# A decode kernel (GQA attention and MLP): the second piece of wo goes through ScalarE's DMA queue

## The chip, the core and the metric

The kernel runs on one core of one Trainium2 chip. The metric is the device time of one execution in microseconds (us). The engines are named as in the profile: PE is TensorE's matmuls and PEld its weight loads, DVE is VectorE, ACT is ScalarE, POOL is GpSimd and SP is SyncE. SPq and ACTq are those engines' sequencers, which also issue DMAs. All times in the text are counted from the start of the profiled span.

## The reference: what is computed

One token x of 512 values passes a layer norm. The result goes two ways, and both are added to x.

```python
xn = _layernorm(x, axis=-1)
return x + _A_ref(xn, A_k_cache, A_v_cache, A_wq, A_wo) + _B_ref(xn, B_w1, B_w2)
```

`_A_ref` is attention of one query position over a cache of 65536 positions: 32 query heads and 8 key/value heads of 128 values (four query heads share a key/value head), softmax, and the product with `wo`, a matrix of 4096 x 512. `_B_ref` is `relu(xn @ w1) @ w2` with 1792 hidden values. Everything is float32. The two caches hold 537 MB, the weights 24 MB.

## The kernel before

The whole kernel is written by hand: every engine has its own program, with semaphore waits where it needs another's result. Two large buffers in SBUF take all loads, `ks` and `vs`, each 128 partitions x 64 KB.

**Start.** SP loads wq into `vs` in two pieces and the first part of K into `ks`; ScalarE loads x twice, 2 KB each. The layer norm and the product with wq give the queries.

**The loop of 32 steps** (8 heads x 4 parts). SP loads a part of K (8 MB) into `ks`, and a part of V (8 MB) into `vs`, as soon as the buffer is free: lines 294 to 299, with the semaphores `k_free` and `v_free`. TensorE multiplies K by the queries (L329), VectorE transposes the scores out of PSUM and takes maxima (L361 to L378), ScalarE makes the exponentials (L407), TensorE multiplies them with V (L345), and VectorE takes the result out of PSUM (L383 to L390). L383 raises `v_free` when the step's last matmul with V is done.

**The end of SP's program** sets the order of the last loads. After the last part of V stand w1 and w2 (3.5 MB each, into `ks`), then a wait for `v_free` to reach 32, and then wo into `vs`. wo is cut into 32 slices of 512 columns, each 2 KB a row, and loaded in six pieces of 16, 8, 4, 2, 1 and 1 slices (`WO`). All this is in one queue. `load_slices` (L158) issues the pieces with `load` (L150), each with a semaphore of its own, and returns for every slice the semaphore of its piece.

**The tail of TensorE.** After the loop it multiplies by w1 (L428), transposes the hidden values (L269), sums the softmax's denominators (L439), scales the attention's output and puts it in order (L453, L461). VectorE makes `sw`, the 32 columns of attention output (L465, L472). Then one chain of products is gathered in PSUM, `gather` at L480 to L487: 14 slices of w2, then the slices 0 to 23 of wo, each waiting for its own piece. L498 copies this sum to SBUF, L501 folds it into `acc_y`, and L510 adds slices 24 to 31 there. L516 adds x, and SP writes y.

```python
for j in range(SLICES):
    row = vs[:, j * D : (j + 1) * D]
    lhsT = sw[:, j : j + 1]
    if j < DIRECT:
        gather(j % CT, lhsT, row, [sw_in, wo_in[j]], last=(j >= DIRECT - CT))
```

TensorE runs its instructions in the order in which they are written, so slice j is multiplied before slice j + 1, whichever piece landed first. ScalarE has nothing to do after its loop (L403 to L420).

Of the kernel before, what the change touches and what calls it, by code (L numbers as in the profile page):

```python
# [30 lines left out]
STEPS = HKV * NP  # L31
# [3 lines left out]
R = HKV  # L35
SLICES = R * G
WQ = [4, 28]
WO = [16, 8, 4, 2, 1, 1]
# [30 lines left out]
def attention_and_mlp_kernel(  # L69
# [29 lines left out]
    te, ve, se, ge, sy = nc.tensor, nc.vector, nc.scalar, nc.gpsimd, nc.sync  # L99
# [4 lines left out]
    def place(name, *shape):  # L104
        return sb.tile([P, *shape], F32, name=name)

    ks = place("ks", NT * KEYS)
    vs = place("vs", NT * KEYS)
# [34 lines left out]
    with tc.tile_critical():  # L143
# [6 lines left out]
        def load(engine, name, dst, src, n=16):  # L150
            sem = nc.alloc_semaphore(name)
            engine.dma_start(dst, src).then_inc(sem, n)
            return sem, n
# [1 line left out]

        x_in = load(se, "x_in", xT, x.rearrange("(p a) -> p a", p=P))

        def load_slices(name, src, counts):  # L158
            marks = []
            for n in counts:  # L160
                cut = slice(len(marks) * D, (len(marks) + n) * D)
                marks += [load(sy, f"{name}{len(marks)}", vs[:, cut], src[:, cut])] * n
            return marks

        def k_part(i):
# [3 lines left out]
        def v_part(i):  # L169
            h, n = divmod(i, NP)  # L170
            src = v[h].rearrange("(p t b) d -> p t (b d)", p=P, b=SUB)
            return src[:, n * NT : (n + 1) * NT, :].rearrange("p t f -> p (t f)")

        wq_in = load_slices("wq", wq.rearrange("h (i r) a f -> (h i) (r a f)", r=R), WQ)
        sy.dma_start(ks, k_part(0)).then_inc(k_in, 16)

# [125 lines left out]
        w1_in = load(sy, "w1_in", t1, w1.rearrange("p a f -> p (a f)"))  # L302
        w2_in = load(sy, "w2_in", t2, w2.rearrange("p j n -> p (j n)"))
        sy.wait_ge(v_free, STEPS)
        wo_in = load_slices("wo", wo.rearrange("h (i r) g f -> (h i) (r g f)", r=R), WO)


        ge.wait_ge(*q_made)
# [13 lines left out]
        with nc.Fori(0, STEPS, engines=[ENG.PE]):  # L322
            te.wait_ge(k_in, 16).then_inc(k_in, -16)
            te.wait_ge(q_in, 1).then_inc(q_in, -1)  # L324
            for s in range(NT):
                pt = (pa, pb)[s // 2 % 2][:, s % 2, :]
                for c in range(CT):
                    at = (s * CT + c) * TW
                    i = te.matmul(pt[32 * c : 32 * c + 32, :], qcur, ks[:, at : at + TW], start=True, stop=True)  # L329
# [12 lines left out]
            n = NT * SUB // WIDE  # L342
# [12 lines left out]
        with nc.Fori(0, HKV, engines=[ENG.DVE]):  # L355
            for n in range(NP):
                for s in range(0, NT, 2):
                    if s == NT - 2:

                        ve.wait_ge(s_tiles, NT // 2).then_inc(k_free, 1)  # L360
                    i = ve.transpose(  # L361
                        tr[:, s * SUB : (s + 2) * SUB, :].rearrange("p b i -> p (b i)"),
                        (pa, pb)[s // 2 % 2].rearrange("p i k -> p (i k)"),
                    )._wait_ge(s_tiles, s // 2 + 1)
# [5 lines left out]
                i = ve.reduce_max(top, tr[:, :, :G].rearrange("p b g -> p g b"), axis=AX.X)  # L370
                if n:
                    ve.drain()
                    i = ve.tensor_max(m, m, mc)  # L373
# [29 lines left out]
        with nc.Fori(0, HKV, engines=[ENG.Activation]):  # L403
            for n in range(NP):
                se.wait_ge(s_bias, 1).then_inc(s_bias, -1)  # L405
                for g in range(G):
                    i = se.activation(  # L407
                        wt[:, :, g], tr[:, :, g], AF.Exp, bias=bias[:, n, g : g + 1],
                        scale=scale, accum_out=part[:, n, g : g + 1],
                    )  # L410
                i.then_inc(s_w, 1)
                if n:
                    se.activation(
                        alpha[:, n : n + 1], bias[:, n - 1, G : G + 1], AF.Exp,
                        bias=bias[:, n, G : G + 1], scale=-1.0,
                    ).then_inc(s_alpha, 1)
            se.wait_ge(s_diff, 1).then_inc(s_diff, -1)
            se.activation(
                fac.rearrange("p n g -> p (n g)"), diff.rearrange("p n g -> p (n g)"), AF.Exp
            ).then_inc(s_alpha, 1)  # L420


        w = t1.rearrange("p (a f) -> p a f", a=A)
# [127 lines left out]
```

## Time and profile before

| | |
|---|---|
| time, median of 3 runs | 1305.26 us (1304.88 to 1305.73) |
| the profiled execution | 1305.38 us |
| its span, first to last instruction | 1303.3 us |
| bytes read from memory | 560.99 MB, 430 GB/s over the span |
| PE busy | 662.4 us (51%) |
| DVE busy | 268.9 us (21%) |
| ACT busy | 75.9 us (6%) |
| granted TensorE clock, mean | 0.734 |

The page gives busy shares of each engine and, in 40 slices of the span, the share of the DMA engines. The DMA lines give for each load its size and the time from its issue to its landing. The timeline lists instructions in order of time: start, duration, engine, line, operation, what it writes and reads, and in brackets how long the engine sat idle before it and what ended that. A granted clock of 0.5 means that TensorE runs at half speed.

### The profile page before, as it was taken

What the parts mean: (1) busy time and instruction counts of PE and PEld (TensorE: products, weight loads), DVE (VectorE), ACT (ScalarE), POOL (GpSimd) and SP (SyncE); (2) the same over time, 40 slices, a digit from 0 to 9 for tenths busy, and PEclk for the clock granted to TensorE, in tenths of its full rate; (3) what the DMA queues carried; (4) which work ended last, traced back from release to release, by engine and by line L of the source; (5) the groups of instructions that cost most, each with busy time, mean ns of one, the idle gap of its engine ahead of it and who ended that gap; (6) DMA issues with size and microseconds to landing.
All of it is one profiled execution on the core that took longest, in us unless ns stands there. A gap on an engine that the chain in (4) does not pass through costs nothing. (4 is left out here: it accounts for less than half of the span.)

```text
span 1303.3 us, 10616 instructions
## 1 busy us (share of the span) xinstructions
PE 662.4 (51%) x4562; PEld 243.2 (19%) x4562; DVE 268.9 (21%) x395; ACT 75.9 (6%) x292; POOL 5.4 (0%) x22
## 2 busy tenths in 40 slices
PE   4355446445445535445545535544544644553657
PEld 2121112112112112111211111221111212111123
DVE  2221122221122222012222112222112222211222
ACT  0000000000000000000000000000000000000000
POOL 0000000000000000000000000000000000000000
PEclk9677687777677677677778677767767666767768
DMA  9999999999999999999999999999999999999998
GB/s 418 419 445 422 447 422 447 420 447 422 440 428 430 438 422 445 424 445 424 445 422 447 422 447 420 443 426 436 432 426 443 424 443 424 445 424 445 422 429 346
DMA packets 10821, 561.06 MB, mean 430 GB/s; under 512 B 1336, under 2 KB 1344, under 8 KB 1728
## 3 DMA queue, kind: packets, MB, share of 16 engines
q1 hardware_dynamic: 10664, 560.99, 99.5%
q8 instruction: 3, 0.05, 0.0%
q10 hardware_dynamic: 152, 0.00, 0.0%
q14 instruction: 2, 0.02, 0.0%
HBM read 560.99 MB, written 0.00 MB: 430 GB/s over the span
## 5 line engine op out<-in xcount | busy, mean ns | idle before, releaser
L345 PE MATMUL acc_o<-vs,wt 128*16 128x512 f32 x2048 | 292.0, 734 | 180.1 <-PEq L341 180.1
L329 PE MATMUL pa<-ks,qcur 128*32 128x512 f32 x1024 | 183.6, 814 | 328.9 <-PEq L324 328.9
L361 DVE STREAM_TRANSPOSE tr<-pa 128x1024 f32<-128x1024 f32 x64 | 80.0, 1250 | 421.4 <-PE pa L329 421.4
L329 PE MATMUL pb<-ks,qcur 128*32 128x512 f32 x1024 | 144.0, 653 | 0.0
L329 PEld LDWEIGHTS pa<-ks,qcur 128*32 128x32 f32 x1024 | 64.3, 133 | 416.2 <-issue 403.7
L345 PEld LDWEIGHTS acc_o<-vs,wt 128*16 128x16 f32 x2048 | 68.9, 113 | 376.4 <-issue 376.4
L407 ACT ACTIVATE wt<-tr,bias 128x128 f32<-128x128 f32 x128 | 64.3, 511 | 1085.3 <-ACTq L405 1085.3
L387 DVE SCALAR_TENSOR_TENSOR acc<-acc,alpha,acc_o 128x512 f32<-128x512 f32 x24 | 17.9, 747 | 352.5 <-PE acc_o L345 352.5
L361 DVE STREAM_TRANSPOSE tr<-pb 128x1024 f32<-128x1024 f32 x64 | 80.0, 1250 | 45.5 <-PE pb L329 45.5
L329 PEld LDWEIGHTS pb<-ks,qcur 128*32 128x32 f32 x1024 | 66.2, 129 | 78.3 <-issue 58.4
L334 PE MATMUL pm<-ident,m 128*4 128x128 f32 x32 | 10.0, 313 | 87.0 <-DVE m L373 66.6
L385 DVE COPY acc<-acc_o 128x512 f32<-128x512 f32 x8 | 5.5, 692 | 118.9 <-PE acc_o L345 118.9
L335 PE MATMUL pm<-dg,ones 4*128 4x4 f32 x64 | 15.0, 302 | 21.4 <-DVE dg L377 21.4
L370 DVE TENSOR_REDUCE mc<-tr 128x4 f32<-128x512 f32 x24 | 24.1, 1006 | 1.8
L334 PEld LDWEIGHTS pm<-ident,m 128*4 128x4 f32 x32 | 2.6, 81 | 116.0 <-DVE m L373 88.4
L407 ACT ACTIVATION_READ_ACCUMULATOR wt<-tr,bias 128x1 f32 x128 | 23.9, 187 | 0.0
L335 PEld LDWEIGHTS pm<-dg,ones 4*128 4x128 f32 x64 | 12.2, 236 | 28.8 <-DVE dg L377 28.8
L336 PE MATMUL pm<-dg,rowg 4*128 4x1 f32 x64 | 14.3, 290 | 0.0
L336 PEld LDWEIGHTS pm<-dg,rowg 4*128 4x128 f32 x64 | 13.0, 249 | 0.0
L278 PE MATMUL pa<-vs,tr 128*8 128x512 f32 x64 | 9.9, 769 | 6.1 <-DMA vs<-wq 4.8
L375 DVE TENSOR_REDUCE mg<-pm 4x1 f32<-4x128 f32 x32 | 8.9, 279 | 13.0 <-PE pm L334 13.0
L378 DVE COPY bias<-pm 128x5 f32<-128x5 f32 x32 | 5.2, 163 | 27.8 <-PE pm L336 27.8
(90 smaller groups left out, 116.6 us busy)
## 6 DMA issues: line engine op xcount, KB each, us to landing
vs<-wq SPq DMA_DIRECT2D x1, 7168.0 KB, 21.4
ks<-w SPq DMA_DIRECT2D x2, 3584.0 KB, 22.1
vs<-wo SPq DMA_DIRECT2D x1, 4096.0 KB, 16.4
vs<-wo SPq DMA_DIRECT2D x1, 2048.0 KB, 20.9
vs<-wq SPq DMA_DIRECT2D x1, 1024.0 KB, 4.9
vs<-wo SPq DMA_DIRECT2D x1, 1024.0 KB, 22.9
ks<-k SPq DMA_DIRECT2D x32, 29.2
vs<-v SPq DMA_DIRECT2D x32, 29.3
```

The lines of the kernel that those rows point to most:

```text
L278: lambda e: e.matmul(pr[32 * c : 32 * c + HKV, :], xs[:, i, :], vs[:, i * 512 : (i + 1) * 512], start=(i < CT), stop=(i >= SLICES - CT),),
L329: i = te.matmul(pt[32 * c : 32 * c + 32, :], qcur, ks[:, at : at + TW], start=True, stop=True)
L334: te.transpose(pm[:G, :P], m, ident)._wait_ge(s_dve, 3).then_inc(s_max, 1)
L335: te.matmul(pm[:, P : P + G], ones[:G, :], dg[:, :G], start=True, stop=True)._wait_ge(s_dve, 4)
L336: te.matmul(pm[:, P + G : P + G + 1], rowg, dg[:, G : G + 1], start=True, stop=True).then_inc(s_max, 1)
L345: mm = te.matmul(acc_o[32 * c : 32 * c + WIDE * G, :], wt[:, i * WIDE : (i + 1) * WIDE, :].rearrange("p b g -> p (b g)"), vs[:, i * 512 : ...
L361: i = ve.transpose(tr[:, s * SUB : (s + 2) * SUB, :].rearrange("p b i -> p (b i)"), (pa, pb)[s // 2 % 2].rearrange("p i k -> p (i k)"),)._ ...
L370: i = ve.reduce_max(top, tr[:, :, :G].rearrange("p b g -> p g b"), axis=AX.X)
L375: ve.reduce_max(mg, pm[:G, :P], axis=AX.X)._wait_ge(s_max, 1)
L385: ve.tensor_copy(flat, acc_o)
L387: ve.scalar_tensor_tensor(flat, flat, alpha[:, n : n + 1], acc_o, op0=ALU.mult, op1=ALU.add)
L407: i = se.activation(wt[:, :, g], tr[:, :, g], AF.Exp, bias=bias[:, n, g : g + 1], scale=scale, accum_out=part[:, n, g : g + 1],)
```

## The change

`load_slices` takes a further argument, the number of a piece that is issued by ScalarE instead of SP. wo is loaded with `other=1`: the second piece, the eight slices from slice 16 on (2 MB, 16 KB a row), is issued by ScalarE, after its loop and after a wait for `v_free`. The other five pieces stay on SP in their order. The call moves behind ScalarE's loop in the text, so that ScalarE's issue comes after its loop; SP's own program keeps its order and its wait. The order of TensorE's work is the same.

```diff
-        def load_slices(name, src, counts):
+        def load_slices(name, src, counts, other=None):
+
             marks = []
-            for n in counts:
+            for i, n in enumerate(counts):
                 cut = slice(len(marks) * D, (len(marks) + n) * D)
-                marks += [load(sy, f"{name}{len(marks)}", vs[:, cut], src[:, cut])] * n
+                engine = se if i == other else sy
+                marks += [load(engine, f"{name}{len(marks)}", vs[:, cut], src[:, cut])] * n
             return marks
...
         sy.wait_ge(v_free, STEPS)
-        wo_in = load_slices("wo", wo.rearrange("h (i r) g f -> (h i) (r g f)", r=R), WO)
...
+        se.wait_ge(v_free, STEPS)
+        wo_in = load_slices("wo", wo.rearrange("h (i r) g f -> (h i) (r g f)", r=R), WO, other=1)
```

## The prediction

> **What bounds the kernel now.** I read the page's slices and queues first, then the DMA issues, then the timeline of the last 30 us with the chain of waits.
>
> ```profile
> DMA  9999999999999999999999999999999999999998
> q1 hardware_dynamic: 10664, 560.99, 99.5%
> ```
>
> The 16 DMA engines are busy to the end, and practically all of it is SP's queue (q1). The packet records say the same more sharply: from 1262 to 1292 us 16.0 transfers are under way in every 2 us. So the last byte can land earlier only if the engines move bytes faster. Loads of one queue land in the order of issue:
>
> ```profile
> vs<-wo SPq DMA_DIRECT2D x1, 4096.0 KB, 16.4
> vs<-wo SPq DMA_DIRECT2D x1, 2048.0 KB, 20.9
> vs<-wo SPq DMA_DIRECT2D x1, 1024.0 KB, 22.9
> vs<-wo SPq DMA_DIRECT2D x1, 512.0 KB, 23.8
> vs<-wo SPq DMA_DIRECT2D x2, 256.0 KB, 24.0
> ```
>
> The six issues begin at 1273.19 and then every 0.37 to 0.49 us. The two weights ahead of them were issued at 1253.40 and 1253.77, and landed 18.0 and 26.1 us later. With the last column this gives the landings: w1 1271.4, w2 1279.9, piece 0 (slices 0 to 15) 1289.6, piece 1 (slices 16 to 23, the one that moves) 1294.5, piece 2 at 1297.0, and the last at 1299.5. Each piece takes a time in proportion to its bytes (9.7, 4.9, 2.5 us): no gap anywhere. TensorE meets them like this:
>
> ```profile
> 1286.69 4.52 PE L483 MATMUL acc_z<-ks,hT 128*1 128x512 f32 x26
> ...
> 1291.05 5.73 PE L483 MATMUL acc_z<-vs,sw 128*1 128x512 f32 x46
> ...
> 1294.54 0.10 PEld L483 LDWEIGHTS acc_z<-vs,sw 128*1 128x1 f32 x6 [0.41 <-DMA vs<-wo]
> ...
> 1296.95 0.69 DVE L498 COPY rows<-acc_z 128x512 f32<-128x512 f32 x1 [9.08 <-PE acc_z L483]
> 1297.69 0.40 PE L501 MATMUL acc_y<-rows,ones 128*1 128x128 f32 x8 [0.91 <-DVE rows L498]
> ...
> 1299.56 0.10 PEld L510 LDWEIGHTS acc_y<-vs,sw 128*1 128x1 f32 x8 [0.23 <-DMA vs<-wo]
> 1300.10 0.29 DVE L516 TENSOR_TENSOR x<-acc_y,x 128x128 f32<-128x128 f32 x1 [2.46 <-PE acc_y L510]
> ```
>
> Columns are start, duration, engine, line. TensorE works through w2's 14 slices, then piece 0, then piece 1, almost without a pause until 1296.78 (1291.05 + 5.73). It waits for piece 1 by less than 0.1 us of lost pace at 1294.54, and for the last piece by 0.12 us at 1299.56 (a group of four that otherwise starts 0.09 us after the one before starts 0.21 after it). So two limits meet here: landings and TensorE's order of slices. TensorE is in order: slice 16 can't run before slice 15. That is what the change disturbs.
>
> **The change part by part.**
>
> *SP loses one issue.* Its four later pieces are issued some 0.45 us earlier. They stand behind 16 us of queued bytes, so this is worth 0. If that cover were gone it would be worth at most the 0.45 us.
>
> *ScalarE gains a wait and one DMA.* Its last activation (L418) ends at 1274.58 and the condition (v_free at 32) was met at 1273.2, so the wait costs nothing; behind it on ScalarE stand only this DMA and the end of the program. An issue lasts 0.33 to 0.44 us in the rows. The load of x at the kernel's start shows the lag: issued by ScalarE at 0.92, its first packets at 1.97, that is 1.05 us. I estimate that piece 1's first rows move at about 1276 (bounds: 1275.6 at once, and 1280 if it takes the 4.7 us that the second load of x took from the end of its issue at 2.46 to its packets at 7.14; that one stood behind the first load's rows in ScalarE's own queue and behind one 56 KB row, and nothing stands ahead here).
>
> *How two queues share an engine.* Before, this happens only in the first 10 us. An engine's eight 16-byte rows of x lie about 0.31 us apart there, each between two 8 KB rows of wq that take 309 ns: the engine alternates row by row. The page's own figure agrees: 2 KB of x took 4.3 us to land beside the first 1024 KB of wq, 4.9 us. Each DMA has 8 rows per engine. Rows take 1.06 us (w2, 28 KB), 1.21 us (piece 0, 32 KB), 0.61 us (piece 1, 16 KB). So from 1276 each row of piece 1 goes between two of SP's. The fast engines have about two rows of w2 left, the slowest about four. Piece 1's eight rows are through after at most eight more rows of SP, which is before the end of piece 0. Piece 1 lands near 1291.5. w2 lands at 1279.9 + 4 x 0.61 = 1282.3 at the latest; its matmuls begin at 1286.69, so those 2.4 us are hidden (cover 4.4 us).
>
> *Piece 0 is the one that pays.* It lands when w2, piece 0 and piece 1 are all through: the sum of bytes that in the run before ended at **1294.5**, instead of 1289.6. Does sharing change the rate? 8 KB rows took 309 ns between the rows of x and 309 to 315 alone at the end, so at most 2% either way; over the 18 us of sharing that bounds it by 0.35 us up or down, and I take 0.
>
> *TensorE.* w2's slices run as before, 1286.69 to about 1291.6. Then TensorE waits some 2.9 us for piece 0 while piece 1 lies ready or nearly so. From 1294.55 it has 24 slices to do instead of 8. The pace at full clock: four instructions, two slices, each 0.43 us (weight loads at 1292.33, 1292.76, 1293.19). 24 slices are 12 such steps; the last starts at 1294.55 + 11 x 0.43 = 1299.28 and lasts 0.59: 1299.87. Before it was 1296.78: **+3.09**. The copy L498, L501 and L510 follow unchanged, only the 0.12 us wait for the last piece goes (it landed at 1299.5, L510 now ends near 1303): **-0.12**. Sum +2.97 us.
>
> *The sum.* The profiled execution took 1305.38 us, its span 1303.3 (2.1 us lie around it); it is 0.12 above the median, 1305.26. 1305.38 + 2.97 = 1308.35, which I give as **1308.3**, against the median +0.23%.
>
> **The TensorE clock in the gap.** In rows: it fell to half at 1279.2 after the window 1275.8 to 1279.2 with TensorE busy 1.50 of 3.40 us, stayed full after 70.9 to 74.3 with 1.43 busy, all matmuls of 512 columns, and fell at 94.8 after 1.13 us.
>
> ```profile
> 1275.80:1279.20 3.40, 1.50 (x12) 0.69 (x6) 2.62 (x6) 0.00 (x0) 1.09 (x1) 1.00 1.02 437
> 1279.20:1282.60 3.40, 3.32 (x16) 3.32 (x16) 0.02 (x1) 0.00 (x0) 0.00 (x0) 0.50 0.98 424
> ...
> 1286.00:1289.40 3.40, 3.40 (x20) 1.17 (x23) 1.04 (x2) 0.00 (x0) 0.00 (x0) 0.50 0.97 414
> 1289.40:1292.80 3.40, 3.40 (x40) 0.70 (x30) 0.00 (x0) 0.00 (x0) 0.00 (x0) 0.99 0.97 410
> ```
>
> (The third number from the end is the granted clock.) The clock moves on a 3.41 us grid. After the change the window 1289.4 to 1292.8 would be busy about 2.2 us and the next, to 1296.2, about 1.7, both above the 1.43 that kept it. So I leave it at full. The Trainium skill ("TensorE: Matmul & The Clock Gate", Part 1) has the clock fall only after a wholly idle window of about 3.4 us; by that the 2.9 us gap is safe and the sum is the same, but the drop at 1279.2 after a window 44% busy speaks against so mild a rule, and it is why the next rival keeps a chance.
>
> **The rivals.**
>
> 1. *The clock falls in the gap.* For: the drops above, and that another execution may have its grid elsewhere. Against: the two windows. From 1294.55 the steps take 0.85 us instead of 0.43 (as at 1287.50 and 1288.35). One cold window of 3.41 us costs half of it, 1.7; a cold stretch to 1299.7 costs 2.6. Time 1310.0 to 1310.9. Chance 0.14.
>
> 2. *Piece 1 is served last*, SP's queue first. Piece 0 lands at 1289.6 as before, the small pieces by 1294.6, piece 1 at 1299.5. Then 8 slices, 4 steps: 1299.55 + 3 x 0.43 + 0.59 = 1301.43 instead of 1296.78, less 0.12: +4.5, 1309.9. Against: the alternating rows of x. Chance 0.04.
>
> 3. *The order in the engines hardly changes: no difference.* Piece 1's rows start late, behind much of piece 0. From a start at about 1280 on (the slowest engine's end of w2), every SP row of 1.21 us that passes first brings piece 0 0.61 us nearer to its old 1289.6. At a start of 1284 piece 0 lands near 1292.5 and piece 1 near 1294 to 1296; the end is then 1305.3 to 1307. For: the second load of x needed 7 us to land. Against: ScalarE is free at 1274.6, and its rows should move four us before the point that decides. If the slowest engines catch up in other executions, piece 0 lands at 1293, TensorE is the limit of the run before too, and the loss shrinks to about 2.2 us, 1307.5: the same side of the bound. The Trainium skill ("DMA: Bandwidth & Descriptors", Queues, rings and completion order) lets an engine take a whole packet of some 9 to 17 descriptors from one queue before it turns to the other. By that piece 1 goes in one turn after w2, and piece 0 still lands at 1294.5; only with a start after 1280 would it come wholly behind piece 0, and the time be 1305.3. The alternating rows above are against it. Chance together 0.17.
>
> 4. *Two queues move bytes faster.* To gain, piece 0 would have to land by 1291.2 and the last by 1297: over 10% more rate in 26 us. Against: engines 99.5% taken, equal 309 ns rows. 1302.5 or less. Chance 0.03.
>
> **How the numbers follow.** Forecast 0.62, rivals 0.14, 0.04, 0.17, 0.03. The forecast's own range is 1307.4 to 1309.2 (0.35 from the rate, the rest from the landing of the slowest engine and from run to run, 1304.88 to 1305.73). A measurement here tells about 0.2%, 2.6 us, from no change, so the bound lies at 1307.87, inside the forecast's lower part: 0.52 of its 0.62 are slower, 0.10 same. Slower 0.52 + 0.14 + 0.04 = 0.70, same 0.27, faster 0.03. The range reaches into rivals 1 and 3: 1306.3 to 1310.3.
>
> **What would show it.** Profile after: the piece of 2048 KB stands at ACTq, with 15 to 18 us to landing; the 4096 KB piece at 21.3 instead of 16.4; a wait of 2.5 to 3 us before slice 0, released by the DMA of wo; L498 starts at 1300.0 relative to the same start; no DMA wait before L510; the last landing unchanged at 1299.5 and the clock at full from 1294.5. Wrong if the 4096 KB piece lands under 19 us (rival 3), if the clock after the gap is 0.5 (rival 1), or if the last landing moves by over 1 us (rival 4).

## The result and the profile after

The changed kernel takes **1310.45 us** in the median of 6 runs (1309.35 to 1311.54), against 1305.30 us before (1304.88 to 1305.73): a ratio of 1.0039, 95% interval 1.0029 to 1.0049. It is slower by 5.2 us, where 3.0 had been forecast and the range ended at 1310.3. The profiled execution took 1310.78 us, its span is 1308.7.

The transfers went as forecast. These are the DMA issues after: size, and time from issue to landing.

```profile
vs<-wo SPq DMA_DIRECT2D x1, 4096.0 KB, 22.7
...
vs<-wo ACTq DMA_DIRECT2D x1, 2048.0 KB, 18.0
...
vs<-wo SPq DMA_DIRECT2D x2, 256.0 KB, 25.9
```

SP's issues begin at 1271.55 here (1273.19 before), so the columns are not compared line by line; added to the issue they are. Piece 0 landed at 1294.24 (before 1289.60), piece 1 at 1290.69 (before 1294.50), the last piece at 1299.28 (before 1299.52). Piece 0 and piece 1 have changed places, and no time was lost or won in the transfers as a whole.

The timeline from the products with the normalised output on:

```profile
1277.48 2.01 PE L458 MATMUL pm<-norm,fins 128*128 128x4 f32 x16 [0.68 <-DVE norm L451]
...
1283.34 4.93 PE L488 MATMUL acc_z<-ks,hT 128*1 128x512 f32 x28
...
1294.38 7.95 PE L488 MATMUL acc_z<-vs,sw 128*1 128x512 f32 x48 [6.11 <-DMA vs<-wo]
...
1302.49 0.69 DVE L503 COPY rows<-acc_z 128x512 f32<-128x512 f32 x1 [17.98 <-PE acc_z L488]
```

(L458 is L453 of before, L488 is L483, L503 is L498.) The wait for piece 0 is there, but it is 6.11 us and not 2.9, and the 48 instructions of the 24 slices last 7.95 us. The chain of waits after says the same in two lines: 22.70 us for the landing, then TensorE.

```profile
1271.55 22.70 DMA vs<-wo
1294.24 0.14 issue
1294.38 8.08 PE acc_z L488 x48
```

The stretches of the clock's grid, the windows of 3.41 us at whose ends the clock changes (TensorE busy is the second number, the granted clock the third from the end):

```profile
1286.10:1289.50 3.40, 2.17 (x16) 0.27 (x8) 0.00 (x0) 0.00 (x0) 0.00 (x0) 1.00 1.06 453
1289.50:1292.90 3.40, 0.00 (x0) 0.00 (x0) 0.00 (x0) 0.00 (x0) 0.00 (x0) 1.00 0.93 398
1292.90:1296.30 3.40, 1.92 (x12) 0.43 (x16) 0.00 (x0) 0.00 (x0) 0.00 (x0) 0.50 0.97 394
1296.30:1299.70 3.40, 3.40 (x20) 0.58 (x16) 0.00 (x0) 0.00 (x0) 0.00 (x0) 0.50 0.38 139
1299.70:1303.10 3.40, 2.63 (x24) 0.38 (x16) 0.61 (x1) 0.00 (x0) 0.00 (x0) 1.00 0.00 0
```

One window passes with TensorE wholly idle, and the clock is at half for the two windows that follow, 1292.9 to 1299.7. From piece 0's landing on, the first 5.3 us of work run at half speed.

The two executions against each other: the gather ended at 1302.33 (1294.38 + 7.95) instead of 1296.78, 5.55 us later, and the profiled times differ by 5.40. With the clock at full, 24 slices take 5.33 us (experiment 3), so the clock has 7.95 - 5.33 = 2.6 us of it in this execution, and the later landing with more slices behind it has the rest.

### The profile page after: what moved, and what is told of

Read it like the earlier page. It is cut to its first block, busy times and chain, and to the rows that moved or that the text cites. A ratio compares the mean times of both kernels' runs of the same rounds, so it can differ in the third digit from the quotient of the medians.

```text
span 1308.7 us, 10617 instructions
## 1 busy us (share of the span) xinstructions
PE 658.4 (50%) x4562; PEld 235.3 (18%) x4562; DVE 268.9 (21%) x395; ACT 75.9 (6%) x292; POOL 5.3 (0%) x22
## 5 line engine op out<-in xcount | busy, mean ns | idle before, releaser
L330 PEld LDWEIGHTS pb<-ks,qcur 128*32 128x32 f32 x1024 | 63.5, 128 | 80.4 <-issue 61.8
L488 PE MATMUL acc_z<-vs,sw 128*1 128x512 f32 x48 | 8.0, 831 | 6.1 <-DMA vs<-wo 6.1
```

The lines of the kernel that those rows point to most:

```text
L488: lambda e: e.matmul(acc_z[32 * c : 32 * c + 1, :], lhsT, row, start=c not in begun, stop=last),
```

## The experiments

The theory after this: the loss has two parts, (a) piece 0 lands 4.6 us later and TensorE, which is in order, then has 24 slices to do instead of 8, and (b) the pause before it lets the clock fall. Rivals: sharing the DMA engines, or the use of ScalarE's queue as such, costs time. All eight kernels were timed in two groups, each with its own runs of the kernel before (1305.24 us for experiments 1 to 4, 1305.32 for 5 to 8).

### 1. All six pieces through ScalarE's queue

```diff
-                engine = se if i == other else sy
+                engine = sy if other is None else se
```

> The kernel after, but all six pieces of wo go through ScalarE's queue, in the same order, so that SP's queue ends with w2. Theory (the loss is the later landing of piece 0, and the TensorE gap that it opens): piece 0 shares only with the rest of w2, so the two together are through at about 1289.6 as in the kernel before, w2 lands up to 4.9 us later (1284.5), pieces 1 to 5 land as before: 1305 to 1306 us, no loss. Rival (a second queue or ScalarE's issue itself costs): as slow as the change or slower, 1310 us or more.

Measured: 1305.40 us (1305.26 to 1306.13), ratio 1.0002 (0.9993 to 1.0011): no difference. The lines of its timeline:

```profile
1283.55 5.18 PE L488 MATMUL acc_z<-ks,hT 128*1 128x512 f32 x28
...
1289.37 3.61 PE L488 MATMUL acc_z<-vs,sw 128*1 128x512 f32 x32 [0.64 <-DMA vs<-wo]
...
1294.19 1.90 PE L488 MATMUL acc_z<-vs,sw 128*1 128x512 f32 x16 [1.20 <-DMA vs<-wo]
...
1296.23 0.69 DVE L503 COPY rows<-acc_z 128x512 f32<-128x512 f32 x1 [11.49 <-PE acc_z L488]
```

8 MB go through ScalarE's queue, part of it beside SP's rows of w2, and nothing is lost: the pieces land in their order (1289.24 and 1294.14) and TensorE waits 0.64 and 1.20 us for them. So neither the queue as such nor this sharing costs time. These lines also show what the one profile of before hid: when TensorE comes to w2 at 1283.5, it waits for piece 0, for piece 1 and at the end for the last two pieces, and the landings set the time.

### 2. The kernel before, with slice 0 waiting for piece 1

```diff
-                gather(j % CT, lhsT, row, [sw_in, wo_in[j]], last=(j >= DIRECT - CT))
+                gather(j % CT, lhsT, row, [sw_in, wo_in[j], wo_in[16]], last=(j >= DIRECT - CT))
```

> The kernel before, all on SP's queue; only TensorE's slice 0 also waits for piece 1 (1294.5). No byte moves otherwise. Theory: this has the whole of the change's loss, since slice 0 begins at 1294.5 here too: 1309.4 to 1311.5 us. Rival (half of the loss comes from the two queues sharing the engines): clearly less than the change, about 1307.5 to 1308.5 us.

Measured: 1310.86 us (1310.04 to 1311.20), ratio 1.0043 (1.0029 to 1.0056), the whole of the change's loss without a second queue.

```profile
1283.49 4.98 PE L483 MATMUL acc_z<-ks,hT 128*1 128x512 f32 x28
...
1294.56 7.99 PE L483 MATMUL acc_z<-vs,sw 128*1 128x512 f32 x48 [6.09 <-DMA vs<-wo]
...
1302.70 0.69 DVE L498 COPY rows<-acc_z 128x512 f32<-128x512 f32 x1 [18.04 <-PE acc_z L483]
```

Start, pause and length of the 24 slices are those of the change to 0.2 us. It is enough that slice 0 begins at 1294.5.

### 3. The change, with TensorE kept busy in the pause

```diff
+        for j in range(FILL):
+            c, i = j % CT, j % FB
+            PE.op(
+                lambda e: e.matmul(
+                    pr[32 * c : 32 * c + 1, :], hT[:, i : i + 1], t2[:, i * D : (i + 1) * D], start=True, stop=True
+                ),
+            )
+
         for j in range(SLICES):
```

with `FILL = 16`.

> The kernel after, plus 16 slices' worth of matmuls (w2's rows again, into a PSUM bank that nobody reads later) between w2's slices and slice 0 of wo, 3.4 us at full clock, so that TensorE is busy in the gap. They add nothing to the output. Theory (about 2 us of the loss are the clock that falls in the gap): the 24 slices run at 0.43 us a step from 1294.4 and the time is 1308.0 to 1308.8 us although TensorE does more. Rival (the clock is not what costs): 1310.4 us or more.

Measured: 1308.24 us (1307.85 to 1308.67), ratio 1.0023 (1.0014 to 1.0033).

```profile
1289.11 4.02 PE L500 MATMUL pa<-ks,hT 128*1 128x512 f32 x30
...
1294.23 5.33 PE L489 MATMUL acc_z<-vs,sw 128*1 128x512 f32 x48 [1.10 <-DMA vs<-wo]
...
1299.70 0.69 DVE L512 COPY rows<-acc_z 128x512 f32<-128x512 f32 x1 [14.90 <-PE acc_z L489]
```

More work, and 2.2 us less time than the change: the 24 slices take 5.33 us instead of 7.95. This is part (b). What is left against the kernel before, 3.0 us, is part (a), and it is the size that the prediction's sum gave it (2.97).

### 4. The change, with piece 1's slices multiplied first

```diff
-        for j in range(SLICES):
+        order = [*range(16, 24), *range(16), *range(24, SLICES)]
+        for at, j in enumerate(order):
```

(and `at` for `j` where the position counts).

> The kernel after, but TensorE multiplies piece 1's eight slices (landed at 1290.7) ahead of piece 0's sixteen. Theory (the order of slices is what hurts): from 1294.3 only 16 slices are left instead of 24, 4 steps fewer, 1.7 us at full clock, and the gap is cut in two, so that the clock falls in fewer executions: 1306.3 to 1308.3 us. Rival (the landing of piece 0 alone sets the time, whatever is left to do): 1310.4 us.

Measured: 1306.66 us (1306.04 to 1309.56), ratio 1.0015 (1.0006 to 1.0024). Of 11 runs eight lie between 1306.0 and 1306.7 and three between 1309.2 and 1309.6.

```profile
1283.78 5.30 PE L488 MATMUL acc_z<-ks,hT 128*1 128x512 f32 x28
...
1291.77 1.90 PE L488 MATMUL acc_z<-vs,sw 128*1 128x512 f32 x16 [2.69 <-DMA vs<-wo]
...
1294.33 3.61 PE L488 MATMUL acc_z<-vs,sw 128*1 128x512 f32 x32 [0.67 <-DMA vs<-wo]
```

In the profiled one (1306.21) TensorE uses the early piece while piece 0 is on its way, and the clock holds. The 3.8 us against the change hold both parts, the order and the clock; experiment 8 parts them. That the three longer ones are those in which the clock fell fits experiment 8, but they were not profiled.

### 5. Piece 2 (1 MB) instead of piece 1

```diff
-WO, other=1)
+WO, other=2)
```

> The kernel after, but piece 2 (1 MB, 8 KB a row) goes through ScalarE's queue instead of piece 1. Theory: w2, piece 0 and piece 1 now stand behind 1 MB more, 2.4 us: piece 0 lands at about 1292, piece 1 at 1297, and 8 slices follow piece 1: 1297.0 + 3 x 0.43 + 0.59 = 1298.9 for the end of the gather (1296.8 in the kernel before), with the clock at full 1307.2 to 1307.6 us. A clock that falls in the gap ahead of piece 0 is paid ahead of piece 1, where there is a pause to absorb most of it. Rival (the loss goes by the bytes moved through ScalarE's queue): half of the change's 5.2 us, 1307.9 us.

Measured: 1307.38 us (1306.81 to 1307.82), ratio 1.0016 (1.0007 to 1.0025).

```profile
1278.98 3.58 PE L458 MATMUL pm<-norm,fins 128*128 128x4 f32 x16 [0.68 <-DVE norm L451]
...
1292.10 3.61 PE L488 MATMUL acc_z<-vs,sw 128*1 128x512 f32 x32 [0.85 <-DMA vs<-wo]
...
1296.93 1.90 PE L488 MATMUL acc_z<-vs,sw 128*1 128x512 f32 x16 [1.22 <-DMA vs<-wo]
```

Piece 0 at 1291.96 and piece 1 at 1296.89, as worked out from 1 MB more in front of them; the gather ends where the sum put it (1296.93 + 1.90 = 1298.83, expected 1298.9). The time follows the landing of the piece that TensorE needs next, plus the slices from there on. The rival's 1307.9 lies just outside all 11 runs.

### 6. The last piece (256 KB) instead of piece 1

```diff
-WO, other=1)
+WO, other=5)
```

> The kernel after, but only the last piece (256 KB, 2 KB a row) goes through ScalarE's queue. Theory: pieces 0 and 1 land 0.6 us later, the rest unchanged at the end: 1305.6 to 1306.0 us. Rival (any use of the second queue in the tail costs microseconds): 1307 us or more.

Measured: 1305.52 us (1305.39 to 1306.19), ratio 1.0003 (0.9994 to 1.0012): nothing that can be told from none, and less than the 0.3 to 0.7 expected. The rival is out. The expectation had counted from the profile of before, where the gather ends at 1296.78; in experiment 1 L503 began already at 1296.23 and L515 then waited 0.19 and 0.51 us for the last two pieces. That slack can take most of the 0.6 us; this is argued, for the one execution profiled here (1306.19) was the slowest of the eleven.

### 7. Half of the filler

As experiment 3 with `FILL = 8`.

> The kernel after with 8 slices' worth of filler matmuls, 1.7 us at full clock, half of the 16 of before: TensorE pauses from about 1290.2 to 1294.3, some 4.1 us. If the clock falls only after a wholly idle window of the 3.41 us grid, a pause of 4.1 us holds one in about one execution in five: 1308.2 to 1308.6 us. If it falls after a window that is busy by less than about 45%, it falls in nearly every execution: 1309.4 to 1310.6 us.

Measured: 1310.05 us (1308.00 to 1311.09), ratio 1.0035 (1.0021 to 1.0049): almost the change itself, as the second of the two theories had it; one run of five, at 1308.00, is as short as with the full filler. In the profile of the run at 1310.05:

```profile
1289.53 2.30 PE L500 MATMUL pa<-ks,hT 128*1 128x512 f32 x14
...
1294.77 7.03 PE L489 MATMUL acc_z<-vs,sw 128*1 128x512 f32 x48 [2.94 <-DMA vs<-wo]
```

The pause was 2.94 us, the very length that the prediction had held to be harmless, and the clock fell: its records show full from 1288.89, half from 1295.72, full again from 1299.13. The window of the grid that ended at 1295.72 began at 1292.30 and had TensorE busy only from 1294.77, 28% of it.

### 8. Piece 1 first, and the small filler

Experiment 4 with the filler of experiment 7 ahead of piece 1's slices.

> The kernel after with piece 1's slices multiplied first and 8 slices' worth of filler matmuls ahead of them (1288.7 to 1290.4), so that no pause is over 2 us. Theory: always at full clock, piece 0's 16 slices begin at 1294.3: 1306.2 to 1306.6 us in all executions, without the spread up to 1309.6 of the same order without filler. Still above the kernel before, since 16 slices follow the landing at 1294.3 where before 8 did. Rival (order and clock are not all): stays at 1307 or more.

Measured: 1306.57 us (1306.29 to 1306.78), ratio 1.0009 (1.0000 to 1.0018). The 11 runs lie within 0.5 us, where experiment 4 had 3.5: in the profiled one no pause is over 1.03 us, and the runs at 1309 are gone.

```profile
1291.74 1.90 PE L489 MATMUL acc_z<-vs,sw 128*1 128x512 f32 x16 [1.03 <-DMA vs<-wo]
...
1294.59 3.62 PE L489 MATMUL acc_z<-vs,sw 128*1 128x512 f32 x32 [0.95 <-DMA vs<-wo]
```

Against experiment 3 this is the price of the order alone, since both profiles have the clock at full from before piece 0's landing on: 1308.24 - 1306.57 = 1.67 us, the 4 steps of 0.43 us that experiment 4's expectation had counted. What remains against before, 1.25 us, fits the order of landing: 16 slices follow 1294.5 instead of 8, again 4 steps, 1.7 us, less what the waits for the later pieces absorb. No run separates this last part. None of the kernels tried beats the one before.

## Why the prediction was wrong, by its steps

**The transfers: right.** The alternation of the queues row by row shows in the packets of piece 1. On an engine its 16 KB rows begin 1.83 us apart beside piece 0: 0.61 + 1.21. w2 landed at 1281.48 (forecast 1282.3 at the latest), piece 1 at 1290.69 (near 1291.5), piece 0 at 1294.24 (1294.5), the last piece at 1299.28 (1299.5). The rivals on the queues (2, 3, 4) fall by these numbers, and by experiment 1. The Trainium skill ("DMA: Bandwidth & Descriptors", Queues, rings and completion order) has an engine take a whole packet of some 9 to 17 descriptors in a turn. This trace shows one row in a turn.

One agreement here is luck. Piece 1's first rows moved at 1276.12, as estimated (about 1276), but ScalarE issued them at 1272.72, 1.9 us earlier than the forecast had it free, and they took 3.40 us to start and not 1.05. The two errors cancel; the landing of piece 0 did not hang on them.

**The order of the slices: right.** +2.97 us was the sum, and with the clock held at full experiment 3 measured 3.0.

**The step that failed: "So I leave it at full."** It stood on a pause of 2.9 us and on two windows that were busy enough. The pause was wrong, and the windows were those of one pause and one position of the grid.

- *The pause.* "w2's slices run as before, 1286.69 to about 1291.6" took one execution's clock for a property of the kernel. In the profile of before, two stretches of the tail ran longer than in the profile of the change: the last products with V (L345, 1.5 us) and the products L453 (1.6 us).

```profile
1263.16 9.91 PE L345 MATMUL acc_o<-vs,wt 128*16 128x512 f32 x64 [5.54 <-PEq L341]
...
1279.28 3.58 PE L453 MATMUL pm<-norm,fins 128*128 128x4 f32 x16 [0.68 <-DVE norm L446]
```

  In the change L345's products took 8.39 us and began 0.24 earlier:

```profile
1262.92 8.39 PE acc_o L346 x64
```

  The clock records say why: in before it was at half until 1268.96, in the change only until 1265.58, and in L453 it was at half in before (from 1279.20) and at full in the change (until 1279.23). Together this is 3.3 us, and TensorE came to w2 at 1283.34 instead of 1286.69. In seven experiments too it came early, at 1283.5 to 1284.6, with L453's row at 1.95 to 1.97 us; only experiment 5 repeats the 3.58 and came at 1286.39. Experiment 2, whose program is the one before but for a wait, came at 1283.49. In the kernel before, an early TensorE need not change the time: in experiment 1, where the pieces land in the same order, it came at 1283.55, waited, and the time was the same. With the change, the earlier TensorE is done, the longer it pauses: 6.11 us instead of 2.9.
- *The windows.* In the profiled execution the grid lay where the forecast had it (1289.47), so there the long pause alone emptied a window. But the grid lies elsewhere in each execution, and a pause of 3 us can fill most of a window: experiment 7's clock fell after 2.94 us of pause. The Trainium skill ("TensorE: Matmul & The Clock Gate", Part 1) has the clock fall after an idle window of about 3.4 us. The profile of the change has one (1289.5 to 1292.9); experiment 7 has none that is wholly idle, and its clock fell all the same. What the rows agree with is the busy share of one window of the grid: the clock fell after 0%, 28% (experiment 7) and 33% (1.13 of 3.40 us in the kernel before), and held after 42% (1.43 of 3.40) of wide matmuls.

All ten profiles of this case bear that out, where the forecast went by three windows. With windows of 3.41 us laid on each profile's own changes of the clock, 635 windows at full clock have TensorE busy under 40%, 457 of them with some work in them. The clock is at half after every one. Of 1080 windows over 41% it is at half after 13, and these 13 all lie where transposes and narrow products run, around 30 us and from 1275 to 1282; the 44% ahead of the fall at 1279.2 is one of them (see the last section). So the 1.43 us that the forecast took for enough were just above the edge. By this share even its own pause was not safe. This is an estimate: 2.95 us of pause leave a window under 41% when over 2.01 us of them fall into it, which is so for 2.95 + 3.41 - 2 x 2.01 = 2.3 of 3.41 us of positions.

So rival 1 happened, at its forecast price (1310.0 to 1310.9, measured 1310.45), with a chance of 0.14 that should have been the largest. Its reason was in part another: it had the grid elsewhere, and the profiled fall came from the longer pause. The range ended at 1310.3, inside that price.

The mechanism of the chosen forecast, and its size, hold for a kernel in which the clock does not fall. The spread of the runs may belong to the same step: 2.2 us with the change, 0.9 before, 0.5 in experiment 8. A clock that stays low for longer in some runs than in others would give such a spread; that each run's time follows its grid is not shown, since only one run of each kernel was profiled.

## What to carry to other kernels

Here, with the DMA engines full, the second queue moved the bytes as a whole no faster (the last piece landed at 1299.28 instead of 1299.52): it decided only which piece was late, and TensorE, which takes the slices in order, paid for the piece that it needs first. Ask then what the consumer does while it waits: here the late piece cost 3.0 us by itself and another 2.2 us through TensorE's clock after the pause. And a start time read from one profile holds only for that execution's clock; before a wait is sized from it, look how early the engine could have come.

## What was not expected of the hardware

Piece 1's first rows moved 3.4 us after ScalarE's issue (1272.72 to 1276.12), while SP's rows of 28 KB, 1.06 us each, were queued on the engines. In the seven experiments that issue a piece of wo on ScalarE it was 3.4 to 3.5 us, for rows of 2 KB to 32 KB. At the kernel's start it was 1.05 us in before. That the queued rows are the cause is not shown, and here nothing hung on it.

Products of many weight loads with few columns did not lift the clock, although they count as busy. In the changed kernel's profile the row for 1279.2 to 1282.6 shows TensorE 3.12 us busy of 3.40 and the clock stays at half for the next window too; it rises only at 1286.1, after a window of which the wide matmuls of w2 fill most. In the ten profiles the clock rose after every window at half clock with TensorE busy over 77%, but for 12, and all 12 hold such products (from 1278.7 to 1286.0).

```profile
1279.20:1282.60 3.40, 3.12 (x17) 3.03 (x16) 0.19 (x1) 0.00 (x0) 0.00 (x0) 0.50 1.01 431
1282.60:1286.00 3.40, 3.40 (x20) 1.22 (x24) 1.03 (x2) 0.00 (x0) 0.00 (x0) 0.50 1.00 429
```
